# Weight blocks every 36 units instead of 34 in a fused attention and feed-forward kernel

## The chip, the cores and the metric

The kernel runs on one core of a Trainium2 chip. The metric is the device time of one execution in microseconds (us). The engines are named as in the profile: PE is TensorE (matrix products; PEld is its loading of weights), DVE is VectorE, ACT is ScalarE, POOL is GpSimd, SP is the queue of SyncE, which issues every DMA of this kernel one after the other.

## What is computed

Attention with queries averaged in pairs, then a feed-forward layer with a tanh-shrink, all in float32:

```python
B, H, S, D = 8, 8, 1152, 64                       # batches, heads, keys, head size
q_pool = q.reshape(B, H, S // 2, 2, D).mean(axis=3)
scores = np.matmul(q_pool, k.transpose(0, 1, 3, 2)) / np.sqrt(D)
scores = scores - scores.max(axis=-1, keepdims=True)
attn = np.exp(scores)
attn = attn / (attn.sum(axis=-1, keepdims=True) + 1e-09)
x = np.matmul(attn, v).transpose(0, 2, 1, 3).reshape(B * S // 2, H * D)   # 4608 x 512
h = x @ w_in                                      # w_in 512 x 2048
out = (h - np.tanh(h)) @ w_out                    # w_out 2048 x 512
```

## The kernel before

There are two stages. The first is the attention, and while it runs the weights of the second stage are prepared on engines that have time to spare. The second is the feed-forward layer, over chunks of 512 tokens; the change doesn't touch its text.

**Pairs and units.** The attention runs over 32 pairs of heads (0 to 31; four pairs make a batch). A pair has two halves of the queries, two heads and nine tiles of keys, so 36 score tiles, and each is a unit. In a unit, `score_unit` makes a tile of scores on PE (two products into `ps_s`, of which there are three buffers) and ACT writes its exponential into `p_f`. After every sixth unit, POOL adds the exponentials into `z` (`z_part`, two additions), and PE multiplies them with the values (`pv`, into `ps_o`), some units later. The sums of `z` over the keys (`z_sums`) go through `ps_s` too.

**What is made ahead.** While the units of a pair run, operands of later pairs are made. In units counted from the start of a pair (the same place in every pair from the third on): at 10 SP loads queries `q_n` and keys `kq` of the pair three ahead; at 22 POOL adds the query pairs into `kq` (`query_sums`); at 26, 28 and 30 ACT rounds `kq` to a high part `x` (`hi_part`); at 34, 0 and 2 DVE subtracts it from `kq`, which gives the low part `kq_l` (`lo_part`); at 1 SP copies the parts into the score operands `t` of the next pair, in ten DMAs (`operands`), at 6 it loads the values `v`, and at 32 it copies `x` into `bd` (`max_queries`).

**Maxima.** The maximum of every row of scores is found ahead, one to two pairs earlier, from rough products: PE writes products of `bd` and `x` into `ps_m` (two buffers), and one unit later DVE reduces each (`mx`, 14 reductions for a pair, at 13, 15, 17, 20, 22, 24, 27, 29, 31, 34, 0, 2, 5 and 7). `max_rows` then reduces them to `nm`, splits it into a rounded and a remaining part in `m2`, PE turns the result (`turn`), ACT copies it out (`mt`), and SP writes it to `m_dram` and reads it back into two rows of `t`.

**Batches.** At 12 in the first pair of the next batch the last sums of a batch are copied out (`z_out`). SP stores them (`z_dram`, at 14) and reads them back as `rec` in four DMAs (`sums`, at 18). DVE takes the reciprocals, and SP spreads them to `r_dram`.

**Weight blocks.** The two weight matrices come as 64-bit patterns of double precision. 32 blocks of 128 x 512 are turned into a high and a low float32 part on the way. `w_block` loads a block (`w_raw`, 512 KB, SP); ACT scales the upper words; five DVE operations follow (clamp, sign, shift, mask, and the lower words); POOL adds; ACT rounds to the high part; POOL subtracts to the low part; SP stores both (`w_hl` to `wi_dram` or `wo_dram`, 512 KB). The places of these steps are a table of offsets in units from the block's start.

**What sets the order.** In the first stage each engine's instructions stay in the order in which the program writes them (`InOrder`, line 27; in the profile all of them have line 37, so tiles tell them apart). The order is written by tables of units: `at` and `first` hold what is issued in each unit, `first` ahead of the unit's scores and `at` behind them. Each engine and SP then work through their own rows strictly in that order, and the first row that waits holds up the rows behind it.

Of the kernel before, what the change touches and what calls it, by code (L numbers as in the profile page):

```python
# [8 lines left out]
F32 = mybir.dt.float32  # L9
F32R = mybir.dt.float32r  # L10
I32 = mybir.dt.int32
AF = mybir.ActivationFunctionType
ALU = mybir.AluOpType
# [30 lines left out]
def kernel(  # L44
# [87 lines left out]
    op0 = ctx.enter_context(tc.tile_pool(name="op0", bufs=1))  # L132
# [3 lines left out]
    t, n = chunks.pop()  # L136
# [4 lines left out]
    with ExitStack() as actx:  # L141
# [3 lines left out]
        op = actx.enter_context(tc.tile_pool(name="op", bufs=1))  # L145
# [12 lines left out]
        U = 4 * KT  # L158
# [18 lines left out]
        at, first = {}, {}  # L177
        end = n_pair * U

        def add(u, f, *args, at=at):  # L180
            at.setdefault(u, []).append(lambda: f(*args))
# [69 lines left out]
        def max_rows(u, pi, steps):  # L251

            w = pairs[pi]
            nm = sm.tile([P, 2, 5], F32, name="nm")
            for h in range(2):
                dve.tensor_reduce(nm[:, h], w.mx[:, 4 * h:4 * h + 5], axis=AX.X, op=ALU.max, negate=True)
            m2 = sm.tile([P, 2, 2, 5], F32R, name="m2")
            dve.tensor_copy(m2[:, 0], nm)
            dve.tensor_tensor(m2[:, 1], nm, m2[:, 0].bitcast(F32), op=ALU.subtract)
            mt = sm.tile([20, P], F32R, name="mt")  # L260
            md = m_dram[w.i]

            def turn():
                ps = w.ps_t = ps_m.tile([P, 2, 512], F32R, name="ps_m")[0:20, 0, 0:P]
                pe.transpose(ps, m2.rearrange("p s h t -> p (s h t)"), ident_r)

            def out():
                act.activation(mt, w.ps_t, AF.Copy)

            def there():  # L270
                sp.dma_start(md[:, 0:10 * P].rearrange("s (r n) -> s r n", n=P), mt.bitcast(F32))

            def back():

                sp.dma_start(w.t2[64:66, :, 0:SQ].bitcast(F32), md.rearrange("s (h n) -> s h n", h=2)[:, :, 0:SQ])
            add(u + steps[0], turn)
            add(u + steps[0] + 1, out, at=first)
            add(u + steps[1], there)
            add(u + steps[2], back)
# [58 lines left out]
        def z_out(u, w, hf, ps):  # L338

            act.activation(w.z_s[:, hf.n * HQ:(hf.n + 1) * HQ], ps[:, 0:HQ], AF.Copy)  # L340
            if hf.n == 1:
                def store():
                    sp.dma_start(x_dram[w.hp, :, w.b * SQ:(w.b + 1) * SQ], w.o_s)
                    sp.dma_start(z_dram[w.b].rearrange("r h a s -> (r h) a s")[:, w.hp], w.z_s[0:P:32])
                add(u + 2, store)
                if w.hp == NP - 1:
                    add(u + 6, lambda: tot.append((w.b, sums(w.b))))
                    if w.b < B - 1:
                        add(u + 22, lambda: reciprocals(dve, *tot[0]))
                        add(u + 25, lambda: spread(sp, *tot.pop(0)))  # L350

        def sums(b):

# [7 lines left out]
        def reciprocals(eng, b, t):  # L361

            eng.scalar_tensor_tensor(t[:, 0], t[:, 0], 1e-9, t[:, 1], op0=ALU.add, op1=ALU.add)
            eng.reciprocal(t[:, 0], t[:, 0])

        def spread(dma, b, t):
            dma.dma_start(r_dram[b].rearrange("h a (x n) -> (h a x) n", n=SQ * NP * 2 // P), t[:, 0])
# [3 lines left out]
        def w_block(u, kind, r, c):  # L371

            top = float.fromhex("0x1.dffffep-96")
            raw = wp.tile([P, WB, 2], I32, name="w_raw", bufs=2)
            lo, hi = raw.bitcast(mybir.dt.uint16)[:, :, 1], raw[:, :, 1]
            ts, stt = dve.tensor_scalar, dve.scalar_tensor_tensor
            t = []

            def begin():

                t[:] = [wp.tile([P, WB], I32, name=f"w_{i}", bufs=1 + (i == 1)) for i in range(3)]
                t.append(wp.tile([P, 2, WB], F32R, name="w_hl", bufs=2))
                act.activation(whole(t[0]), whole(hi), AF.Copy, scale=2.0 ** -112)

            def whole(x):
                return x.bitcast(F32)

            def store():
                src = t[3].bitcast(F32)
                if kind == 0:  # L390
                    f = c // P
                    sp.dma_start(wi_dram[f:f + WB // P, :, :, r].rearrange("f p s m -> p s f m"),
                                 src.rearrange("p s (f m) -> p s f m", m=P))
                else:
                    sp.dma_start(wo_dram[r, :, :, c:c + WB], src)
            sp.dma_start(raw.rearrange("p n w -> p (n w)"),
                         (w_in, w_out)[kind][r * P:(r + 1) * P, 2 * c:2 * (c + WB)])
            for i, op in ((12, begin),
                          (17, lambda: ts(whole(t[0]), whole(t[0]), -top, top, op0=ALU.max, op1=ALU.min)),
                          (20, lambda: ts(t[1], t[0], -0x80000000, None, op0=ALU.bitwise_and)),  # L400
                          (22, lambda: stt(t[1], t[0], 3, t[1], op0=ALU.logical_shift_left, op1=ALU.bitwise_or)),
                          (25, lambda: ts(t[2], t[1], -0x800000, None, op0=ALU.bitwise_and)),
                          (27, lambda: stt(whole(t[2]), lo, 2.0 ** -36, whole(t[2]), op0=ALU.mult, op1=ALU.mult)),
                          (29, lambda: pool.tensor_tensor(whole(t[1]), whole(t[1]), whole(t[2]), op=ALU.add)),
                          (34, lambda: act.activation(t[3][:, 0], whole(t[1]), AF.Copy)),
                          (36, lambda: pool.tensor_tensor(t[3][:, 1], whole(t[1]), whole(t[3][:, 0]), op=ALU.subtract)),
                          (40, store)):
                add(u + i, op)

        blocks = []  # L410
# [3 lines left out]
            for r in range(f // P, (f + WB) // P):  # L414
                blocks.append((1, r, 0))
        for i, blk in enumerate(blocks):
            u = U // 2 + 34 * i
            add(u, w_block, u, *blk)

        tot = []  # L420
# [17 lines left out]
        for pi in range(n_pair):  # L438
            u = pi * U
            units = dict(load=-98, query_sums=-86, hi_q=-82, hi_k=-80, max_queries=-76, lo_q=-74, lo_k=-72, operands=-35, load_v=-30)  # L440
            row, steps = -26, (5, 8, 14)
            parts = [-60 + i * 33 // 14 for i in range(14)]
            step = 2
            if pi == 0:
                units.update(load=-70, query_sums=-60, hi_q=-59, hi_k=-58, max_queries=-57, lo_q=-56, lo_k=-55, operands=-54,
                             load_v=-50)
                row, steps, step = -32, (2, 4, 5), 0
                parts = [-46 + i for i in range(14)]
            if pi == 1:
                v0 = -U  # L450
                units.update(load=v0 - 69, query_sums=v0 - 31, hi_q=v0 - 30, hi_k=v0 - 29, max_queries=v0 - 28, lo_q=v0 - 27,
                             lo_k=v0 - 26, operands=v0 - 25)
                parts = [v0 + 2 + i * 20 // 14 for i in range(14)]
                row, steps, step = v0 + 23, (2, 4, 8), 0
            if pi == 2:
                units.update(query_sums=-80, hi_q=-76, hi_k=-74, max_queries=-70, lo_q=-66, lo_k=-64)
                parts = [-49 + i * 23 // 14 for i in range(14)]
            add(u + units["load"], load, pi)
            add(u + units["query_sums"], query_sums, pi, dve if pi < 2 else pool)
            for what, f in (("hi", hi_part), ("lo", lo_part)):  # L460
                add(u + units[what + "_q"], f, pi, 0, SQ)
                add(u + units[what + "_k"], f, pi, SQ, 2 * SQ)
                add(u + units[what + "_k"] + step, f, pi, 2 * SQ, KQ)
            add(u + units["max_queries"], max_queries, pi)
            for x, part in zip(parts, spots):
                add(u + x, max_part, u + x, pi, *part)
            add(u + units["operands"], operands, pi)
            add(u + units["load_v"], load_v, pi)
            add(u + row, max_rows, u + row, pi, steps)
# [97 lines left out]
    for ci, (t0, n) in enumerate(chunks):  # L567
        x_h, x_l, _ = xs
        po = []
        for fc in range(NF):  # L570
# [15 lines left out]
            def rest(po=po, g=g, fc=fc, t0=t0, nt=n // P, ci=ci):  # L586
                if fc == 0:
                    po += [ps_o.tile([P, DM], F32, name="ps_o") for _ in range(nt)]
                second(po, *g, nt, fc)
                if fc == NF - 1:  # L590
                    store(po, t0, nt, ci)
# [39 lines left out]
```

## Time and profile before

| what | us |
|---|---|
| median of three runs | 1827.98 |
| lowest and highest of them | 1825.22 and 1828.62 |
| the profiled execution | 1825.99 |
| its span, from the first instruction to the last | 1824.2 |
| PE busy | 1741.4 |
| DVE busy | 1403.8 |
| ACT busy | 1084.0 |
| POOL busy | 1050.4 |

The attention ends near 990 us in the span, and the feed-forward layer takes the rest. A group of instructions is shown with its count, its busy time, the mean of one in ns and the idle time of its engine just ahead of it, with what ended that idle time. In a row of the timeline the first number is the start in us, the second the length, and brackets give the idle time ahead of it and who ended it. A row of busy times in stretches has a bracketed count behind each engine's time, and then the granted PE clock, the busy share of the DMA engines, and GB/s.

### The profile page before, as it was taken

What the parts mean: (1) busy time and instruction counts of PE and PEld (TensorE: products, weight loads), DVE (VectorE), ACT (ScalarE), POOL (GpSimd) and SP (SyncE); (2) the same over time, 40 slices, a digit from 0 to 9 for tenths busy, and PEclk for the clock granted to TensorE, in tenths of its full rate; (3) what the DMA queues carried; (4) which work ended last, traced back from release to release, by engine and by line L of the source; (5) the groups of instructions that cost most, each with busy time, mean ns of one, the idle gap of its engine ahead of it and who ended that gap; (6) DMA issues with size and microseconds to landing.
All of it is one profiled execution on the core that took longest, in us unless ns stands there. A gap on an engine that the chain in (4) does not pass through costs nothing. (4 is left out here: it accounts for less than half of the span.)

```text
span 1824.2 us, 28257 instructions
## 1 busy us (share of the span) xinstructions
PE 1741.4 (95%) x9920; PEld 1306.6 (72%) x9920; DVE 1403.8 (77%) x1823; ACT 1084.0 (59%) x2473; POOL 1050.4 (58%) x756
## 2 busy tenths in 40 slices
PE   4999999999999989999998999999999999999998
PEld 3666666766676666666665777878787888788887
DVE  5776767677767777776741899988998899888897
ACT  2555555656565555555554655666666666666676
POOL 2666778777787767777864274353534444433433
PEclk9999999999999999999999999999999999999999
DMA  8767787878878676878763821020101010100000
GB/s 211 201 175 219 180 227 196 221 196 219 228 207 232 168 213 181 212 212 227 196 169 131 313 58 64 6 65 6 64 9 61 13 57 18 44 14 34 27 15 21
DMA packets 104141, 242.29 MB, mean 133 GB/s; under 512 B 18112, under 2 KB 43328, under 8 KB 104000
## 3 DMA queue, kind: packets, MB, share of 16 engines
q1 hardware_dynamic: 104000, 240.49, 47.7%
q8 instruction: 78, 1.28, 0.3%
q14 instruction: 63, 0.52, 0.1%
HBM read 109.64 MB, written 36.42 MB: 80 GB/s over the span
## 5 line engine op out<-in xcount | busy, mean ns | idle before, releaser
L37 DVE TENSOR_REDUCE mx<-ps_m 128x2 f32<-128x768 f32 x448 | 405.5, 924 | 258.2 <-PE ps_m L37 257.9
L37 ACT ACTIVATE p_f<-ps_s 128x288 f32<-128x288 f32 x1152 | 418.0, 411 | 193.6 <-PE ps_s L37 169.7
L37 PE MATMUL ps_s<-t 128*128 128x288 f32 (+1 forms) x2304 | 447.6, 313 | 15.1 <-ACT p_f L37 9.1
L544 POOL TENSOR_TENSOR g_lo<-g_s,g_hi 128x512 fp32r<-128x512 f32 (+1 forms) x160 | 209.2, 1308 | 414.3 <-ACT g_hi L543 360.0
L37 PEld LDWEIGHTS ps_s<-t 128*128 128x128 f32 (+1 forms) x2304 | 357.2, 191 | 120.0 <-issue 90.2
L37 POOL TENSOR_TENSOR z<-p_f 128x576 f32<-128x576 f32 x192 | 289.7, 1509 | 159.5 <-PE ps_s L37 112.0
L526 PE MATMUL ps_h<-x,wi 128*128 128x512 f32 (+1 forms) x1440 | 325.0, 370 | 1.4 <-DVE g_s L541 1.4
L37 PE MATMUL ps_o<-p_f,v 128*64 128x288 f32 x2304 | 325.7, 419 | 0.0
L37 POOL TENSOR_TENSOR z<-z,p_f 128x576 f32<-128x576 f32 x192 | 290.4, 1512 | 17.9 <-ACT p_f L37 3.2
L526 PEld LDWEIGHTS ps_h<-x,wi 128*128 128x128 f32 x1440 | 254.9, 188 | 53.4 <-ACT g_u L532 1.8
L551 PE MATMUL ps_o<-wo,g_hi 128*128 128x512 f32 x1008 | 275.7, 392 | 4.2 <-ACT g_hi L543 3.8
L37 PE MATMUL ps_m<-x,bd 128*128 128x384 f32 x864 | 237.7, 355 | 32.0 <-DVE mx L37 17.5
L37 PEld LDWEIGHTS ps_o<-p_f,v 128*64 128x64 f32 x2304 | 149.8, 138 | 114.8 <-issue 29.8
L551 PEld LDWEIGHTS ps_o<-wo,g_hi 128*128 128x128 f32 x1008 | 186.8, 188 | 46.3 <-ACT g_hi L543 7.4
L543 ACT ACTIVATE g_hi<-g_s 128x512 fp32r<-128x512 f32 (+1 forms) x160 | 94.3, 590 | 153.8 <-DVE g_s L542 151.5
L37 PEld LDWEIGHTS ps_m<-x,bd 128*128 128x128 f32 x864 | 143.5, 196 | 49.6 <-DVE mx L37 27.9
L539 DVE SCALAR_TENSOR_TENSOR g_w<-g_w,g_u 128x512 f32<-128x512 f32 (+1 forms) x160 | 172.6, 1079 | 0.0
L551 PE MATMUL ps_o<-wo,g_lo 128*128 128x512 f32 x504 | 160.1, 393 | 5.6 <-POOL g_lo L544 5.4
L532 ACT ACTIVATE g_u<-ps_h 128x512 f32<-128x512 f32 (+1 forms) x160 | 87.5, 547 | 119.5 <-PE ps_h L526 119.0
L542 DVE COPY_PREDICATED g_s<-g_m,g_t 128x512 f32<-128x512 int32 (+1 forms) x160 | 133.3, 833 | 14.7 <-DVE g_s L541 0.5
L540 DVE SCALAR_TENSOR_TENSOR g_w<-g_s,g_w 128x512 f32<-128x512 f32 (+1 forms) x160 | 129.3, 808 | 18.8 <-ACT g_s L534 2.2
L541 DVE SCALAR_TENSOR_TENSOR g_s<-g_s,g_w 128x512 f32<-128x512 f32 (+1 forms) x160 | 126.5, 790 | 17.0 <-ACT g_t L533 0.5
(60 smaller groups left out, 1887.8 us busy)
## 6 DMA issues: line engine op xcount, KB each, us to landing
t<-x SPq DMA_DIRECT2D x64, 432.0 KB
q_n<-in_q_dram SPq DMA_DIRECT2D x32, 576.0 KB
kq<-in_k_dram SPq DMA_DIRECT2D x32, 576.0 KB
t<-kq_l SPq DMA_DIRECT2D x64, 288.0 KB
t<-x SPq DMA_DIRECT2D x64, 288.0 KB
v<-in_v_dram SPq DMA_DIRECT2D x32, 576.0 KB
bd<-x SPq DMA_DIRECT2D x64, 144.0 KB
t<-kq_l SPq DMA_DIRECT2D x64, 144.0 KB
```

What stands on the lines that cost most here:

```text
L37: ins = self.tc.keep_in_program_order(f(*args, **kwargs))
L526: nc.tensor.matmul(h, wi[fc][:, w, c], x[:, c, 0:n], start=(j == 0), stop=(j == len(mm) - 1))
L532: nc.scalar.activation(u, h, AF.Square)
L539: nc.vector.scalar_tensor_tensor(w, w, PL, u, op0=ALU.mult, op1=ALU.mult)
L540: nc.vector.scalar_tensor_tensor(w, s2, P2, w, op0=ALU.add, op1=ALU.mult)
L541: nc.vector.scalar_tensor_tensor(s1, s1, P1, w, op0=ALU.add, op1=ALU.mult)
L542: last = nc.vector.copy_predicated(s1, m.bitcast(I32), th).ins
L543: nc.scalar.activation(g_h, s1, AF.Copy)
L544: nc.gpsimd.tensor_tensor(g_l, s1, g_h.bitcast(F32), op=ALU.subtract)
L551: nc.tensor.matmul(po[j], g[:, ts], wo[fc][:, w], start=(fc == 0 and i == 0), stop=(fc == NF - 1 and i == 2))
```

## The change

A block now starts every 36 units, the length of a pair, at unit 0 of each pair: before, it started every 34 units, from unit 18, so that its steps moved two units earlier in the pair with each block. The offsets of its steps change too. The five DVE operations now stand at 13, 15, 18, 22 and 25 of each pair, POOL's two at 27 and 32, and ACT's two at 11 and 30. The store stands at 36, which is unit 0 of the next pair, behind the load of the next block (also at unit 0) and ahead of the ten copies of the operands (unit 1).

In `max_rows` the rounding of `nm` moves from DVE to ACT, and the subtraction behind it is put three units later. `max_rows` itself starts one unit earlier, and what follows the turn keeps its place. The reciprocals of a batch move from unit 34 to 28, and their spreading from 37 to 31.

```diff
             m2 = sm.tile([P, 2, 2, 5], F32R, name="m2")
-            dve.tensor_copy(m2[:, 0], nm)
-            dve.tensor_tensor(m2[:, 1], nm, m2[:, 0].bitcast(F32), op=ALU.subtract)
+            act.activation(m2[:, 0], nm, AF.Copy)
+
+            def rest():
+                dve.tensor_tensor(m2[:, 1], nm, m2[:, 0].bitcast(F32), op=ALU.subtract)
+            add(u + steps[0] - 3 if steps[0] > 3 else u + 1, rest, at=first)
...
-                        add(u + 22, lambda: reciprocals(dve, *tot[0]))
-                        add(u + 25, lambda: spread(sp, *tot.pop(0)))
+                        add(u + 16, lambda: reciprocals(dve, *tot[0]))
+                        add(u + 19, lambda: spread(sp, *tot.pop(0)))
...
-            for i, op in ((12, begin),
-                          (17, lambda: ts(whole(t[0]), whole(t[0]), -top, top, op0=ALU.max, op1=ALU.min)),
+            for i, op in ((11, begin),
+                          (13, lambda: ts(whole(t[0]), whole(t[0]), -top, top, op0=ALU.max, op1=ALU.min)),
...
-                          (40, store)):
+                          (36, store)):
...
-            u = U // 2 + 34 * i
+            u = U * i
...
-            row, steps = -26, (5, 8, 14)
+            row, steps = -27, (6, 9, 15)
```

The next rows show what stands in three queues, around pair 21. `w_raw` is the load of a block, `wo_dram<-w_hl` the store of one, `t...` the copies of the operands.

SP, from the last copy of the operands in pair 21 on, before:

```order
L37 DMA t_0_122<-x 64x1728
L37 DMA r_dram<-rec 128x36
L37 DMA v<-in_v_dram 128x1152
L37 DMA w_raw<-in_moe_w_out_dram 128x1024
L37 DMA q_n<-in_q_dram 128x1152
L37 DMA kq<-in_k_dram 128x1152
L37 DMA x_dram<-o_s 128x576
L37 DMA z_dram<-z_s 4x576
L37 DMA wo_dram<-w_hl 128x1024
L37 DMA m_dram<-mt 2x10x128
L37 DMA t_0_122<-m_dram 2x2x576
L37 DMA bd_125<-x 64x576 x2
```

The same stretch of SP after the change:

```order
L37 DMA t_0_122<-x 64x1728
L37 DMA v<-in_v_dram 128x1152
L37 DMA q_n<-in_q_dram 128x1152
L37 DMA kq<-in_k_dram 128x1152
L37 DMA x_dram<-o_s 128x576
L37 DMA z_dram<-z_s 4x576
L37 DMA m_dram<-mt 2x10x128
L37 DMA t_0_122<-m_dram 2x2x576
L37 DMA bd_125<-x 64x576 x2
L37 DMA w_raw<-in_moe_w_out_dram 128x1024
L37 DMA wo_dram<-w_hl 128x1024
L37 DMA t_1_123<-kq_l 64x1152
```

The block's load and store have moved from among the loads of `v`, `q_n` and `kq` to a place between `bd` and the first copy of the next operands; the same two rows stand there in every pair from the second on.

POOL in pair 21, up to the query sums (`kq`), before:

```order
L37 TENSOR_TENSOR w_7341<-w_7341,w_7342 128x512
L37 TENSOR_TENSOR z<-p_f 128x576
L37 TENSOR_TENSOR z<-z,p_f 128x576
L37 TENSOR_TENSOR w_hl<-w_7341,w_hl 128x512
L37 TENSOR_TENSOR z<-p_f 128x576
L37 TENSOR_TENSOR z<-z,p_f 128x576
L37 TENSOR_TENSOR z<-p_f 128x576
L37 TENSOR_TENSOR z<-z,p_f 128x576
L37 TENSOR_TENSOR kq<-q_n 128x576
```

POOL in pair 21 from the query sums on, after the change:

```order
L37 TENSOR_TENSOR kq<-q_n 128x576
L37 TENSOR_TENSOR z<-p_f 128x576
L37 TENSOR_TENSOR z<-z,p_f 128x576
L37 TENSOR_TENSOR w_7540<-w_7540,w_7541 128x512
L37 TENSOR_TENSOR z<-p_f 128x576
L37 TENSOR_TENSOR z<-z,p_f 128x576
L37 TENSOR_TENSOR w_hl<-w_7540,w_hl 128x512
```

Before, the block's two operations on POOL stood at another place in each pair, here well ahead of the query sums; now they stand behind them in every pair.

DVE in pair 20, around the reciprocals (`rec`), before:

```order
L37 TENSOR_SCALAR w_7340<-w_7340 128x512
L37 TENSOR_REDUCE mx<-ps_m 128x2
L37 TENSOR_SCALAR w_7341<-w_7340 128x512
L37 TENSOR_REDUCE mx<-ps_m 128x2
L37 TENSOR_TENSOR kq_l<-kq,x 128x576
L37 SCALAR_TENSOR_TENSOR rec<-rec 128x36
L37 RECIPROCAL rec<-rec 128x36
L37 SCALAR_TENSOR_TENSOR w_7341<-w_7340,w_7341 128x512
L37 TENSOR_REDUCE mx<-ps_m 128x2
L37 TENSOR_TENSOR kq_l<-kq,x 128x576
```

The same place after the change:

```order
L37 TENSOR_REDUCE mx<-ps_m 128x2 x2
L37 TENSOR_SCALAR w_7194<-w_7193 128x512
L37 TENSOR_REDUCE mx<-ps_m 128x2
L37 SCALAR_TENSOR_TENSOR w_7194<-w_raw,w_7194 128x512
L37 TENSOR_REDUCE mx<-ps_m 128x2
L37 SCALAR_TENSOR_TENSOR rec<-rec 128x36
L37 RECIPROCAL rec<-rec 128x36
L37 TENSOR_REDUCE mx<-ps_m 128x2 x3
L37 TENSOR_TENSOR kq_l<-kq,x 128x576
```

The reciprocals now stand three reductions earlier, and the block's operations have left the stretch in which the low parts `kq_l` are made.

More of the change, by code (lines that the diff above doesn't have):

```diff
@@ L397, in w_block @@
                          (w_in, w_out)[kind][r * P:(r + 1) * P, 2 * c:2 * (c + WB)])
-            for i, op in ((12, begin),
-                          (17, lambda: ts(whole(t[0]), whole(t[0]), -top, top, op0=ALU.max, op1=ALU.min)),
[L400 to L406, printed above, removed]
-                          (40, store)):
+            for i, op in ((11, begin),
+                          (13, lambda: ts(whole(t[0]), whole(t[0]), -top, top, op0=ALU.max, op1=ALU.min)),
+                          (15, lambda: ts(t[1], t[0], -0x80000000, None, op0=ALU.bitwise_and)),
+                          (18, lambda: stt(t[1], t[0], 3, t[1], op0=ALU.logical_shift_left, op1=ALU.bitwise_or)),
+                          (22, lambda: ts(t[2], t[1], -0x800000, None, op0=ALU.bitwise_and)),
+                          (25, lambda: stt(whole(t[2]), lo, 2.0 ** -36, whole(t[2]), op0=ALU.mult, op1=ALU.mult)),
+                          (27, lambda: pool.tensor_tensor(whole(t[1]), whole(t[1]), whole(t[2]), op=ALU.add)),
+                          (30, lambda: act.activation(t[3][:, 0], whole(t[1]), AF.Copy)),
+                          (32, lambda: pool.tensor_tensor(t[3][:, 1], whole(t[1]), whole(t[3][:, 0]), op=ALU.subtract)),
+                          (36, store)):
                 add(u + i, op)
```

## The prediction

> **What bounds the kernel now.** I read the busy times first, then the busy times by stretch, then what PE waits for, and last the queues of SP and POOL, because the order shows rows moved there.
>
> ```profile
> span 1824.2 us, 28257 instructions
> PE 1741.4 (95%) x9920; PEld 1306.6 (72%) x9920; DVE 1403.8 (77%) x1823; ACT 1084.0 (59%) x2473; POOL 1050.4 (58%) x756
> L37 ACT ACTIVATE p_f<-ps_s x1152: 382/410/453, 38.0 to 989.8; 128x288 f32<-128x288 f32 x192
> 38.00:164.40 126.40, 119.71 (x779) 84.57 (x780) 92.40 (x112) 68.86 (x184) 82.92 (x58) 0.99 0.72 190
> 164.40:907.00 742.60, 718.50 (x4901) 502.02 (x4901) 537.33 (x671) 428.36 (x1153) 560.26 (x379) 1.00 0.78 209
> 907.00:990.20 83.20, 79.86 (x534) 53.39 (x534) 28.94 (x44) 45.55 (x128) 57.14 (x41) 0.99 0.60 164
> ```
>
> The exponentials run from 38 to 990 us: that is the attention, and the change is there. Its units are counted by them, so a pair starts at every 36th. The three stretches are pairs 0 to 3 (126.4 us), 4 to 28 (742.6 us, 29.70 each) and 29 to 31 (83.2 us). PE is busy 718.5 of 742.6 us, so PE bounds the stage, but DMA (the share ahead of the last number in a row) is close behind: 0.72 and 0.78 of its time.
>
> ```profile
> PE ps_m L37 <- DVE mx L37: 21.1, 22, 1.9
> PE ps_s L37 <- ACT p_f L37: 4.9, 14, 0.9
> 343.40:371.90 28.50, 28.33 (x197) 19.95 (x197) 20.05 (x26) 17.06 (x46) 23.14 (x16) 1.00 0.81 214
> 371.90:401.00 29.10, 28.48 (x198) 20.01 (x197) 22.53 (x28) 17.05 (x46) 23.37 (x16) 1.00 0.72 196
> 637.50:669.50 32.00, 29.15 (x199) 20.06 (x198) 22.77 (x28) 17.02 (x47) 21.37 (x16) 1.00 0.71 193
> ```
>
> From 70 to 936 us PE waits 21.1 us for maxima and 4.9 us for exponentials. The other three rows are pairs 10, 11 and 20. As a block moves two units in each pair, the run before has tried nearly every place. Pair 20, whose block falls among the low parts, takes 32.0 us; pairs 10 and 11, whose DVE operations stand between units 13 and 25, take 28.5 and 29.1.
>
> **The change, part by part.**
>
> *DVE's places.* After the change the first operations stand as in pair 11 and the last as in pair 10, so DVE should hold up PE nowhere. The block's rounding on ACT comes at unit 30, where it stood in pair 11:
>
> ```profile
> 396.10 0.68 ACT L37 ACTIVATE x<-kq 128x576 fp32r<-128x576 f32 x1
> 396.68 0.62 ACT L37 ACTIVATE w_hl<-w 128x512 fp32r<-128x512 f32 x1
> 397.65 0.83 PE L37 MATMUL ps_s<-t 128*128 128x288 f32 x4 [0.45 <-ACT p_f L37]
> ```
>
> It follows ACT's third high part directly, and PE waits 0.45 us. So this part alone would give pair 11's 29.1 us, 0.6 less than 29.70.
>
> *The rounding of the maxima.*
>
> ```profile
> L37 DVE CAST m<-nm x32: 173/902/1242, 25.4 to 941.6; 128x10 fp32r<-128x10 f32 x32
> L37 ACT ACTIVATE mt<-ps_m x32: 249/251/268, 27.0 to 946.6; 20x128 fp32r<-20x128 f32 x32
> ```
>
> DVE loses 32 operations of 902 ns in the middle case; ACT gets 32 of about 250 ns (by its nearest row). They lie in the pause in which PE does `pv` and `z_sums`, so I cost them at nothing; without that cover it would be 32 × 0.25 = 8 us. Nor do I count DVE's freed time: 29.1 us holds already that DVE stops nobody.
>
> *The load and the store of a block.* This is the part that decides. The store now stands ahead of the ten copies of the operands, and `q_n` behind them. The run before has this order in pairs 12 and 13, when pair 11's and pair 12's stores came late:
>
> ```profile
> 399.09 0.64 SPq L37 DMA_DIRECT2D wi_dram<-w_hl  x1
> 399.83 1.81 SPq L37 DMA_DIRECT2D t<-kq_l  x2
> ...
> 412.05 2.01 SPq L37 DMA_DIRECT2D q_n<-in_q_dram  x1
> 421.12 1.42 POOL L37 TENSOR_TENSOR kq<-q_n 128x576 f32<-128x576 f32 x1 [4.97 <-DMA q_n<-in_q_dram]
> 422.57 0.68 ACT L37 ACTIVATE x<-kq 128x576 fp32r<-128x576 f32 x1 [1.40 <-POOL kq L37]
> 428.06 0.52 SPq L37 DMA_DIRECT2D wo_dram<-w_hl  x1
> 449.62 1.43 POOL L37 TENSOR_TENSOR kq<-q_n 128x576 f32<-128x576 f32 x1 [2.62 <-DMA q_n<-in_q_dram]
> ```
>
> From the issue of the store to the query sums that `q_n` releases: 421.12 − 399.09 = 22.03 us, and 449.62 − 428.06 = 21.56 us; mean 21.8. POOL stands idle for 4.97 us, and ACT waits 1.40 us with exponentials queued behind it. The other half of the way, from the query sums to the next store, is POOL's own row. In pair 28 it has the order that every pair gets now:
>
> ```profile
> 895.64 1.42 POOL L37 TENSOR_TENSOR kq<-q_n 128x576 f32<-128x576 f32 x1 [3.26 <-DMA q_n<-in_q_dram]
> 897.03 1.42 POOL L37 TENSOR_TENSOR z<-p_f 128x576 f32<-128x576 f32 x1
> ...
> 899.89 1.28 POOL L37 TENSOR_TENSOR w<-w,w 128x512 f32<-128x512 f32 x1
> 901.11 1.43 POOL L37 TENSOR_TENSOR z<-p_f 128x576 f32<-128x576 f32 x1
> ...
> 903.99 1.28 POOL L37 TENSOR_TENSOR w_hl<-w,w_hl 128x512 fp32r<-128x512 f32 x1
> 905.30 0.33 SPq L37 DMA_DIRECT2D wo_dram<-w_hl  x1
> ```
>
> Seven operations without a pause, 905.30 − 895.64 = 9.66 us, and SP issues the store 0.03 us after they end. So a ring closes: store, operands, `v`, `q_n`, query sums, `z`, the block's sum, `z`, the block's low part, next store. Each step stands behind the one ahead of it in an in-order queue, and the ring is passed once per pair: 21.8 + 9.66 = 31.4 us. Before, it was open, since the block moved on in each pair. PE alone needs 29.1 us, so the ring sets the pace, and PE waits in between for ACT, which waits at unit 26 for the query sums and at unit 30 for the block's sum.
>
> How it closes in: a store 1.9 us ahead of a pair's start, as in pair 12 (399.09 against 401.0), puts the query sums at 20.1 us of the pair. POOL's sum of the block then ends 1.42 + 2.9 + 1.28 = 5.6 us later, at 25.7, but ACT comes to unit 30 near 24.8 (pair 11: 396.68 − 371.9). ACT and PE so lose 0.9 us beside the 0.45, and the pair takes 29.9. The next store comes 20.1 + 9.66 = 29.8 us after the pair's start, 0.1 ahead of the next one, and the next query sums at 21.7: ACT's high part is late too, by 1.4 + 21.7 − 21.6 = 1.5 us, since pair 12 could bear it at 21.6 (422.57 − 401.0). That pair takes 28.5 + 0.45 + 1.5 + 0.9 = 31.4, the ring's own length, and so it stays.
>
> Bounds: in pair 11 the store stands behind the ten copies; the first copy was issued at 367.90, and the query sums started at 388.51, so 20.6 us hold the same bytes in another order; with 9.66 that makes 30.3 us. The longest way is 22.03 plus pair 11's POOL part, 399.09 − 388.51 = 10.58: 32.6 us.
>
> ```profile
> 367.90 1.10 SPq L37 DMA_DIRECT2D t<-kq_l  x2
> 388.51 1.41 POOL L37 TENSOR_TENSOR kq<-q_n 128x576 f32<-128x576 f32 x1 [2.17 <-DMA q_n<-in_q_dram]
> 399.09:421.12 22.03, 21.52 (x149) 15.32 (x146) 15.69 (x23) 11.45 (x32) 12.91 (x8) 1.00 0.92 236
> ```
>
> I take 31.4, since its DMA half was measured twice in this very order. The last row says why it can't shrink much: DMA is 92% busy on that way, at 236 GB/s.
>
> The Trainium skill sees this otherwise: "DMA: Bandwidth & Descriptors", section Bandwidth, has 341 GB/s for a transfer of 1 MB. The 4.36 MB from store to `q_n` would take 12.8 us by it, an estimate, and the ring 22.4 us: it would not bind, which is the third case below. The row's 236 GB/s at 92% busy speaks against it.
>
> *The reciprocals.*
>
> ```profile
> 420.98 1.85 DVE L37 TENSOR_REDUCE mx<-ps_m 128x2 f32<-128x768 f32 x2 [1.34 <-PE ps_m L37]
> 423.10 2.42 SPq L37 DMA_DIRECT2D rec<-z_dram  x4
> 428.43 1.40 DVE L37 SCALAR_TENSOR_TENSOR rec<-rec 128x36 f32<-128x36 f32 x1
> 429.86 0.38 DVE L37 RECIPROCAL rec<-rec 128x36 f32<-128x36 f32 x1
> ```
>
> In pair 12 SP ends issuing their data at 425.52. Their new place is between the two reductions of the first row, near 421.9, so DVE would stand for 3.6 us or more, then work 1.8 us, with three reductions behind it. PE can fill its two `ps_m` buffers meanwhile, so of some 5.4 us 2 to 3.5 reach PE, seven times. Where the ring sets the pace, this fits into PE's waits or is made good in the next pair: I take 0, with 0 and 7 × 3.5 = 24 as ends. Moving them away from unit 34 gains nothing that the 29.1 us don't hold already: pair 11 has none.
>
> *Start and end.* In pair 0 the maxima of two pairs lie close together, and DVE has six reductions in a row without a pause:
>
> ```profile
> 47.27 5.27 DVE L37 TENSOR_REDUCE mx<-ps_m 128x2 f32<-128x768 f32 x6
> 976.45 1.26 DVE L37 TENSOR_TENSOR x_f<-x_f,x_r 128x512 f32<-128x512 f32 x1 [32.20 <-DMA x_r<-r_dram]
> ```
>
> Block 0's five operations now fall there. They come to some 4 us, of which I put 3 on PE (0 to 5). Its maxima are two pairs' worth, so PE's work there stays. In pairs 1 to 3 the ring closes in. Pair 1 has a store that is not late yet and two maxima more than pair 11: 29.9 us. Pair 2 takes 29.1, pair 3 between this and 31.4, so 30.6. Pair 0 takes the 32 us from 38 to 70 and the 3. At the end two blocks lie in pairs 30 and 31, where DVE otherwise stands idle for 32.20 us; the last store comes between the fetches of the first chunk: 1 us (0 to 2). The feed-forward stage keeps its work: 0, its first chunk's order differs slightly (−1 to 1).
>
> *The sum.* Pairs 0 to 3: 35 + 29.9 + 29.1 + 30.6 = 124.6 for 126.4, −1.8. Pairs 4 to 28: 25 × 31.4 = 785 for 742.6, +42.4. End: +1. That is +41.6 on the profiled execution's 1825.99 us: 1867.6. The median of the runs is 2.0 above the profiled one, so I predict 1870 us. With the ring at 30.3 and 32.6 us it would be 1842 and 1900.
>
> **The rivals.** A difference of less than 0.2% can't be told from none.
>
> *The fixed places win.* If the ring doesn't bind (the transfers go faster when nothing else is in flight) and the reciprocals find their data, pairs 4 to 28 take 29.1 us: 727.5, −15.1. With −1.8 and +1 that is −16, 1812 us. For it: pairs 10 and 11. It holds as long as store to `q_n` takes under 29.1 − 9.7 = 19.4 us; the smallest in the rows is 20.6.
>
> *The reciprocals wait, the ring doesn't.* As just now, with 7 × 2.7 = 19 us back: 1831 us, from 1819 to 1845. PE's clock makes the upper end likelier:
>
> ```profile
> 587.95 0.23 PE L37 MATMUL ps_m<-ident_r,m 128*20 128x128 f32 x1 [1.86 <-DVE mx L37]
> 588.60:592.00 3.40, 3.40 (x14) 2.15 (x16) 1.12 (x2) 1.29 (x3) 2.44 (x2) 0.50 0.98 375
> ```
>
> A pause of 1.86 us in pair 18 was followed by 3.4 us at half clock, 1.7 us more. The Trainium skill ("TensorE: Matmul & The Clock Gate", section Why this matters for your kernels) tells of drops only after pauses over about 3 us; here a shorter one did it.
>
> **How the numbers follow.** The ring 0.64, the reciprocals alone 0.14, the win 0.22. The win gives faster; the reciprocals alone split into 0.02 faster, 0.04 same, 0.08 slower. So 0.24 faster, 0.04 same, 0.72 slower. The ring's own range is 1842 to 1900. To hold eight in ten the range reaches to 1812 below, which leaves half of the win out (0.11), and to 1895 above (0.04).
>
> **What would show it.** Right: the query sums' row has 28 starts some 31.4 us apart, POOL waits for `q_n` about 4 us in every pair, ACT's high part waits for POOL, SP's store waits for POOL's `w_hl`, and PE's wait for maxima is nearly gone while that for exponentials grows from 4.9 us to over 50. Wrong: query sums 29 us apart, with little idle time ahead of them; then the DMA half was mis-sized.

## The result, and the profile after

The changed kernel takes 1868.08 us (median of 4 runs, 1867.14 to 1870.75), against 1828.30 us for the kernel before (median of 4, 1825.22 to 1831.85). The ratio is 1.0229, with a 95% interval from 1.0213 to 1.0244: the change makes the kernel 2.3% slower. The profiled execution of the changed kernel took 1867.14 us, its span 1865.0 us.

The first lines of the page of the changed kernel:

```profile
span 1865.0 us, 28261 instructions
PE 1754.3 (94%) x9920; PEld 1316.6 (71%) x9920; DVE 1385.2 (74%) x1791; ACT 1095.7 (59%) x2505; POOL 1051.7 (56%) x756
```

Its busy times by stretch (length of the stretch, busy time of each engine with its number of instructions, granted PE clock, DMA share, GB/s). The stretches are again pairs 0 to 3, 4 to 28, and 29 to 31:

```profile
38.20:167.50 129.30, 119.52 (x779) 85.60 (x780) 90.56 (x112) 70.21 (x189) 85.97 (x58) 0.99 0.71 185
167.50:946.40 778.90, 729.74 (x4902) 511.56 (x4901) 507.46 (x639) 435.92 (x1175) 556.88 (x378) 0.97 0.75 198
946.40:1029.20 82.80, 80.39 (x534) 53.48 (x534) 34.39 (x43) 46.77 (x131) 57.81 (x41) 0.98 0.60 167
```

| stretch | before, us | after, us | difference |
|---|---|---|---|
| ahead of pair 0 | 38.0 | 38.2 | +0.2 |
| pairs 0 to 3 | 126.4 | 129.3 | +2.9 |
| pairs 4 to 28 | 742.6 | 778.9 | +36.3 |
| pairs 29 to 31 | 83.2 | 82.8 | −0.4 |
| the rest of the span | 834.0 | 835.8 | +1.8 |

So the loss lies in pairs 4 to 28, now 31.16 us each. The engines hardly have more work there: DVE has 30 us less, ACT 8 us more, with the roundings of the maxima, and PE is busy 11 us longer with the same products, at a granted clock of 0.97. Above all they wait more. The waits of PE in pairs 1 to 29 (total us, times, longest):

```profile
PE ps_s L37 <- ACT p_f L37: 33.6, 35, 2.2
PE ps_m L37 <- DVE mx L37: 15.4, 7, 2.9
PE ps_m L37 <- ACT mt L37: 5.1, 29, 0.2
```

The wait for exponentials has grown from 4.9 to 33.6 us. The wait for maxima has shrunk, from 22 waits to 7: one for each batch whose reciprocals were moved. What the other engines and SP wait for, in the whole span:

```profile
POOL kq L37 <- DMA q_n<-in_q_dram: 174.7, 29, 27.3
ACT x L37 <- POOL kq L37: 54.8, 22, 8.0
DVE rec L37 <- DMA rec<-z_dram: 47.7, 7, 7.7
ACT w L37 <- DMA w_raw<-in_moe_w_in_dram: 6.2, 1, 6.2
SPq L37 <- POOL w_hl L37: 137.3, 26, 9.9
```

POOL waits 174.7 us for `q_n` (55.4 before), and SP 137.3 us for POOL's `w_hl` (39.3 before). Each of the two stands behind the other. The timeline of SP and POOL in pair 18 (which starts at 600.9) shows one round:

```profile
601.52 0.64 SPq L37 DMA_DIRECT2D wi_dram<-w_hl  x1
602.26 1.82 SPq L37 DMA_DIRECT2D t<-kq_l  x2
...
613.86 0.64 SPq L37 DMA_DIRECT2D v<-in_v_dram  x1
614.55 2.00 SPq L37 DMA_DIRECT2D q_n<-in_q_dram  x1
622.00 1.40 POOL L37 TENSOR_TENSOR kq<-q_n 128x576 f32<-128x576 f32 x1 [6.70 <-DMA q_n<-in_q_dram]
...
630.71 1.79 POOL L37 TENSOR_TENSOR w_hl<-w,w_hl 128x512 fp32r<-128x512 f32 x1
632.53 0.64 SPq L37 DMA_DIRECT2D wi_dram<-w_hl  x1
```

From a store to the query sums 622.00 − 601.52 = 20.48 us, from there to the next store 10.53, together 31.0: the pair's length.

The second part of the loss is in the seven pairs with reciprocals. In pair 20, which starts at 663.5, DVE stands 7.66 us for their data, and PE pauses twice, as the timeline of SP, DVE and PE shows:

```profile
687.12 2.90 SPq L37 DMA_DIRECT2D rec<-z_dram  x4
691.65 0.29 DVE L37 SCALAR_TENSOR_TENSOR rec<-rec 128x36 f32<-128x36 f32 x1 [7.66 <-DMA rec<-z_dram]
687.59 1.16 PE L37 MATMUL ps_s<-z,ones 128*32 128x288 f32 x12 [1.83 <-ACT p_f L37]
693.23 1.01 PE L37 MATMUL ps_m<-x,bd 128*128 128x384 f32 x2 [1.78 <-DVE mx L37]
```

From 688.9 us on PE runs at half clock for 10.2 us (the 0.50 in this row of the busy times):

```profile
688.90:699.10 10.20, 8.42 (x31) 5.80 (x31) 5.84 (x8) 3.64 (x9) 9.33 (x7) 0.50 0.52 132
```

Pairs 4, 8, 12, ... 28 take 34.7 us in the mean, the other 18 take 29.8. After a pair with reciprocals the next takes 29.1 to 29.6, since POOL and SP come ahead of PE in the long pause: the next store leaves 2.3 to 5.1 us ahead of the next pair, where the one in pair 18 left 0.7 us behind its pair's start. Then the ring closes again, and in three of the six batches the pairs are back at 31.0 to 31.6 us before the next reciprocals.

### The profile page after: what moved, and what is told of

The parts are those of the page before. It is cut to its first block, busy times and chain, and to the rows that moved or that the text cites. A ratio compares the mean times of both kernels' runs of the same rounds, so it can differ in the third digit from the quotient of the medians.

```text
span 1865.0 us, 28261 instructions
## 1 busy us (share of the span) xinstructions
PE 1754.3 (94%) x9920; PEld 1316.6 (71%) x9920; DVE 1385.2 (74%) x1791; ACT 1095.7 (59%) x2505; POOL 1051.7 (56%) x756
## 3 DMA queue, kind: packets, MB, share of 16 engines
q8 instruction: 78, 1.28, 0.3%
## 4 chain that ended last, share of the span: by engine, by line
PE 62%; DVE 10%; DMA 10%; ACT 7%; POOL 6%; issue 3%; SPq 2%; DVEq 0%; POOLq 0%; ACTq 0%
PE ps_s L37 18%; PE ps_o L37 13%; PE ps_o L554 12%; PE ps_h L529 12%; PE ps_m L37 7%; DMA q_n<-in_q_dram 3%; DMA z_dram<-z_s 2%; DVE g_s L544 2%; DVE g_s L545 2%; SPq L37 2%; DMA x_f<-x_dram 2%; ACT p_f L37 2%; DVE g_w L543 2%; POOL x L124 1%; POOL x_f L118 1%
## 5 line engine op out<-in xcount | busy, mean ns | idle before, releaser
L37 PEld LDWEIGHTS ps_s<-t 128*128 128x128 f32 (+1 forms) x2304 | 361.7, 193 | 131.9 <-issue 84.9
L37 PE MATMUL ps_o<-p_f,v 128*64 128x288 f32 x2304 | 330.8, 424 | 0.0
L37 PE MATMUL ps_m<-x,bd 128*128 128x384 f32 x864 | 243.7, 363 | 32.3 <-DVE mx L37 16.9
L37 PEld LDWEIGHTS ps_o<-p_f,v 128*64 128x64 f32 x2304 | 151.5, 139 | 118.1 <-issue 34.7
L542 DVE SCALAR_TENSOR_TENSOR g_w<-g_w,g_u 128x512 f32<-128x512 f32 (+1 forms) x160 | 180.0, 1125 | 0.0
L37 POOL TENSOR_TENSOR kq<-q_n 128x576 f32<-128x576 f32 x30 | 42.7, 1424 | 174.7 <-DMA q_n<-in_q_dram 174.7
```

The source lines that it names most:

```text
L37: ins = self.tc.keep_in_program_order(f(*args, **kwargs))
L542: nc.vector.scalar_tensor_tensor(w, w, PL, u, op0=ALU.mult, op1=ALU.mult)
```

## The experiments

The theory: the ring through SP and POOL sets the pace, and the reciprocals' waits come on top. The main rival: the reciprocals make the loss, with PE's pauses and its clock, and the ring only echoes them. The first four runs separate the two edits.

**The store behind the copies.** The ring is opened, and nothing else is touched:

```diff
-                          (36, store)):
+                          (38, store)):
```

> The changed kernel, but the store of a block stands behind the ten copies of the operands instead of ahead of them; the reciprocals stay at unit 28. The way from the store to the query sums then holds only v, q_n and kq's load, and the ring is far shorter than a pair. Ring theory (ring and reciprocals both cost, the ring more): the 18 pairs of 4 to 28 without reciprocals fall to 29.1 us each, the 7 with them to 32 to 34.5, sum 755, so 1838 us (1828 to 1848). Rival (the waits for the reciprocals' data make the whole loss, the ring is only their echo): nothing is gained beside the shift itself, 1858 to 1868 us.

Measured: 1816.51 us, ratio to the kernel before 0.9938 (0.9920 to 0.9955). Moving this one DMA gives 51.6 us, more than the theory had said and against the rival. Pairs 4 to 28 in the busy times:

```profile
163.50:893.40 729.90, 712.53 (x4902) 500.55 (x4901) 528.97 (x640) 431.91 (x1175) 563.97 (x375) 1.00 0.80 210
```

A batch's reciprocals in pair 20, which starts at 631.0, and the transfers ahead of them in the timeline:

```profile
637.89 0.65 SPq L37 DMA_DIRECT2D wi_dram<-w_hl  x1
640.02 1.17 SPq L37 DMA_DIRECT2D q_n<-in_q_dram  x1
649.14 2.41 SPq L37 DMA_DIRECT2D rec<-z_dram  x4
654.63 0.91 DVE L37 SCALAR_TENSOR_TENSOR rec<-rec 128x36 f32<-128x36 f32 x1 [3.09 <-DMA rec<-z_dram]
```

And DVE's waits for them, with SP's for `w_hl`, in the whole span:

```profile
DVE rec L37 <- DMA rec<-z_dram: 14.5, 7, 3.1
SPq L37 <- POOL w_hl L37: 8.8, 1, 8.8
```

A pair takes 29.2 us, with reciprocals or without. My 32 to 34.5 us for the former was wrong: with the ring open, SP issues the reads of `rec` 18.1 us into the pair (649.14 − 631.0) where it needed 23.6 (687.12 − 663.5), and DVE waits 14.5 us in all instead of 47.7. PE feels up to 0.8 us of it, three times. So most of the waits for the reciprocals' data was itself the ring's work: SP came late. The last row shows that the ring is open: SP waits for `w_hl` once, and no longer in nearly every pair (26 times, 137.3 us).

**The reciprocals back.** The ring stays closed; reciprocals and spreading stand at 34 and 37 again:

```diff
-                        add(u + 16, lambda: reciprocals(dve, *tot[0]))
-                        add(u + 19, lambda: spread(sp, *tot.pop(0)))
+                        add(u + 22, lambda: reciprocals(dve, *tot[0]))
+                        add(u + 25, lambda: spread(sp, *tot.pop(0)))
```

> The changed kernel, but reciprocals and their spreading back at units 34 and 37 as before the change; the store stays ahead of the ten copies. Ring theory: no long pause lets a store leave early any more, so all of pairs 4 to 28 run at the ring's length, 31.0 to 31.6 us, 775 to 790 in sum: 1862 to 1876 us, no better than the changed kernel, although the waits for the reciprocals' data are gone. Rival (the reciprocals make the loss): the pairs with them fall from 34.7 to 29.8 us like the others, 745 in sum: 1832 to 1838 us.

Measured: 1860.19 us, ratio 1.0179 (1.0158 to 1.0200). The rival's 1832 to 1838 is refuted; the time lies 2 us under the theory's range, whose pace was a little high. Its pairs 4 to 28 in the busy times:

```profile
167.80:934.10 766.30, 718.92 (x4902) 506.22 (x4901) 513.91 (x638) 436.21 (x1175) 553.29 (x376) 0.99 0.76 200
```

PE's wait for exponentials in pairs 1 to 29, and SP's for `w_hl` in the whole span:

```profile
PE ps_s L37 <- ACT p_f L37: 45.5, 49, 2.1
SPq L37 <- POOL w_hl L37: 147.6, 31, 7.0
```

And the round of pair 18 in the timeline:

```profile
595.66 0.64 SPq L37 DMA_DIRECT2D wi_dram<-w_hl  x1
608.94 1.79 SPq L37 DMA_DIRECT2D q_n<-in_q_dram  x1
616.47 1.40 POOL L37 TENSOR_TENSOR kq<-q_n 128x576 f32<-128x576 f32 x1 [7.02 <-DMA q_n<-in_q_dram]
625.18 1.80 POOL L37 TENSOR_TENSOR w_hl<-w,w_hl 128x512 fp32r<-128x512 f32 x1
627.00 0.64 SPq L37 DMA_DIRECT2D wi_dram<-w_hl  x1
```

No wait for maxima is left, and the pairs take 766.3 / 25 = 30.65 us. Over the 24 rounds in this stretch the way from store to query sums takes 20.25 us in the mean (19.3 to 21.2), and back 10.37 (10.0 to 10.6): 30.6 us. That this is the pair's length says little by itself, since every version has one store in each pair, and its rounds are as long as its pairs in the mean. What shows the closed ring is that neither half holds slack. SP comes from the store at 595.66 to `q_n` at 608.94 with no more than 0.11 us between two of its rows. POOL starts the query sums when `q_n` has landed, its seven operations leave 0.16 us idle in the mean, and the next store follows the end of `w_hl` by 0.02 us. Of the 32 stores, 31 wait for `w_hl`.

So the ring sets the pace alone here, and the changed kernel's other 7.9 us come from the reciprocals, which cost that only as long as the ring is closed: with the ring open, the next run has 1817.5 us without their move, and the one above 1816.5 with it.

**Both edits together.**

> Both edits of the two runs beside it: store behind the ten copies, reciprocals back at 34 and spreading at 37. If ring and reciprocals are the whole loss: pairs 4 to 28 take 29.1 us each, 727.5 in sum for 778.9, so 1817 us (1810 to 1823), below the kernel before. Rival (a third cause, as the DMA's load as a whole or DVE's new places): 1830 us or more.

Measured: 1817.52 us, ratio 0.9941 (0.9924 to 0.9959), as the two causes demand; no third is needed. Pairs 4 to 28 in the busy times, 29.18 us each:

```profile
164.80:894.40 729.60, 713.88 (x4903) 500.73 (x4902) 530.96 (x637) 430.50 (x1176) 565.04 (x375) 1.00 0.81 210
```

**A shorter ring.** The reciprocals are back, the store stays ahead of the copies, and `q_n` and the keys go ahead of `v` in SP's row:

```diff
-            units = dict(load=-98, query_sums=-86, ...
+            units = dict(load=-103, query_sums=-86, ...
```

> Reciprocals back at 34 and 37, store ahead of the ten copies as in the change, but q_n and the keys are loaded five units earlier, so that they stand ahead of v in SP's row. The ring stays closed but loses v's 576 KB, 2.5 us at 236 GB/s: 28.5 to 29 us, just under what PE needs. Ring theory: 1816 to 1830 us. Rival (the ring isn't what sets the pace): the same as with the reciprocals moved back alone, within 5 us.

Measured: 1814.11 us, ratio 0.9923 (0.9902 to 0.9944). Pairs 4 to 28 in the busy times:

```profile
161.20:890.30 729.10, 713.42 (x4903) 500.85 (x4902) 523.62 (x639) 431.52 (x1176) 565.01 (x376) 1.00 0.79 210
```

POOL's wait for `q_n` in one of them, by the timeline:

```profile
469.02 1.41 POOL L37 TENSOR_TENSOR kq<-q_n 128x576 f32<-128x576 f32 x1 [1.51 <-DMA q_n<-in_q_dram]
```

The way from store to query sums falls from 20.25 to 18.66 us in the mean, 1.6 us where I had expected 2.5, and the pair to 29.16, the length that it has with the ring open. The loss is gone although the store still stands ahead of the copies and SP still waits for `w_hl` 31 times (108.7 us): 766.3 − 729.1 = 37.2 us of the 46 between the medians. In the two profiled executions the rest lies at the start, where pair 0 begins 6.7 us earlier (33.2 against 39.9 us); that was not followed up.

**A longer ring, closed and open.** One more POOL addition per block, into a tile that nobody reads any more:

```diff
+                          (29, lambda: pool.tensor_tensor(whole(t[2]), whole(t[1]), whole(t[2]), op=ALU.add)),
```

With the ring closed and the reciprocals back:

> Reciprocals back and the store ahead of the ten copies, as in the run with the reciprocals moved back alone (1860 us, pairs of 30.65 us, ring 20.25 + 10.37 = 30.6 us), and one more POOL addition per block, whose result nobody reads, between the block's sum and its low part: 1.28 us by its row, inside the ring. Ring theory: the pair grows by the whole 1.28 us, to 31.9; 25 pairs give 32, so 1892 us (1880 to 1900). Rival (POOL's and SP's waits are only symptoms; POOL is idle 7 us in each pair and takes up 1.3 more): within 5 us of 1860.

Measured: 1901.72 us, ratio 1.0406 (1.0380 to 1.0432). With the ring open:

> The same added POOL operation, but with the store behind the ten copies, so the ring is open. Ring theory: POOL idles and the operation costs nothing: 1817 us (1813 to 1823). Rival (POOL's work itself is what PE waits for): 1840 us or more.

Measured: 1816.73 us, ratio 0.9943 (0.9923 to 0.9964). The stretch of pairs 4 to 28, closed and then open:

```profile
169.30:981.20 811.90, 732.54 (x4902) 516.50 (x4901) 507.72 (x638) 435.59 (x1175) 586.34 (x401) 0.97 0.71 189
```

```profile
163.70:893.00 729.30, 713.23 (x4902) 500.33 (x4901) 534.89 (x637) 430.96 (x1175) 600.93 (x401) 1.00 0.81 211
```

The same instruction costs 41.5 us in the one kernel and nothing in the other. That is the ring shown by itself: in this stretch POOL stands idle for `q_n` in both kernels, 195.5 us in the closed one and 45.0 in the open one, and still each addition counts in full where it lies ahead of the next store in the ring. It even cost more than its 1.28 us: the pair grew from 30.65 to 32.48. POOL's part of the round grew by 1.45 us (to 11.81) and the transfers' part by 0.36 (to 20.62); PE's granted clock fell from 0.99 to 0.97, with pauses of up to 5.1 us. Why the transfers' part grew isn't settled.

**The rounding alone.** The kernel before, with only the rounding of the maxima on ACT and what belongs to it:

```diff
-            dve.tensor_copy(m2[:, 0], nm)
-            dve.tensor_tensor(m2[:, 1], nm, m2[:, 0].bitcast(F32), op=ALU.subtract)
+            act.activation(m2[:, 0], nm, AF.Copy)
...
-            row, steps = -26, (5, 8, 14)
+            row, steps = -27, (6, 9, 15)
```

> The kernel before, with only the rounding of the maxima moved to ACT, the subtraction put later and the row of maxima started one unit earlier; blocks, stores and reciprocals as before. If the rounding is a part without cost: 1828 us (1822 to 1831). If DVE's freed 0.9 us per pair is what wins in the open versions: 1818 us or less. If ACT's added operation holds up exponentials: up to 8 us more, 1836.

Measured: 1819.63 us, ratio 0.9965 (0.9951 to 0.9979): between the two values, a small gain. And the opposite, the open ring with the rounding on DVE:

> Open ring and reciprocals back (1817.5 us), but the rounding of the maxima on DVE as before the change, with the subtraction right behind it and the row of maxima at its old unit. What is left of the change is the blocks' fixed places. The rounding alone gave 6 us over the kernel before. If places and rounding help PE against the same waits for maxima, fixed places need no rounding: 1817 to 1820 us. If the two add up: 1823 to 1826 us, and fixed places alone give next to nothing.

Measured: 1816.34 us, ratio 0.9942 (0.9922 to 0.9963). PE's wait for maxima in pairs 1 to 29 of the first, and pairs 4 to 28 of the second:

```profile
PE ps_m L37 <- DVE mx L37: 16.3, 18, 1.6
```

```profile
165.50:894.80 729.30, 713.54 (x4903) 500.56 (x4902) 537.13 (x663) 430.08 (x1151) 564.96 (x376) 1.00 0.80 211
```

The two parts don't add up: both go against the same waits for maxima (21.1 us before, 16.3 with the rounding alone), and where the blocks have their fixed places the rounding is worth nothing.

**A version that beats both.** Open ring, reciprocals back, and two edits at places that the traces had shown: block 0 begins at unit 18, and the block's rounding on ACT leaves unit 30, where it follows the third high part:

```diff
-                          (30, lambda: act.activation(t[3][:, 0], whole(t[1]), AF.Copy)),
-                          (32, lambda: pool.tensor_tensor(t[3][:, 1], whole(t[1]), whole(t[3][:, 0]), op=ALU.subtract)),
+                          (33, lambda: act.activation(t[3][:, 0], whole(t[1]), AF.Copy)),
+                          (34, lambda: pool.tensor_tensor(t[3][:, 1], whole(t[1]), whole(t[3][:, 0]), op=ALU.subtract)),
...
-            u = U * i
+            u = U * i if i else U // 2
```

> Open ring (store behind the ten copies), reciprocals back, and two more edits: block 0 starts at unit 18 of pair 0, so that ACT doesn't wait 5.6 us for its data there (pair 0 from 37.8 to 32 us, -5), and the block's rounding on ACT moves from unit 30 to 33, behind the pause of the exponentials, with POOL's low part at 34 (PE's 0.45 us per pair gone, 28 pairs, -13). From 1817.5 us: 1800 us (1796 to 1808). If the rounding's place isn't what PE waits for: 1812.

Measured: 1797.88 us, ratio 0.9844 (0.9821 to 0.9867): 1.6% faster than the kernel before. Its pair 0, and its pairs 4 to 28:

```profile
38.30:70.30 32.00, 31.14 (x184) 23.91 (x185) 24.67 (x30) 17.50 (x46) 18.50 (x13) 1.00 0.73 192
159.80:875.30 715.50, 711.16 (x4902) 500.25 (x4901) 509.87 (x639) 428.52 (x1175) 570.56 (x376) 1.00 0.82 215
```

Pairs of 28.62 us instead of 29.18 (14 us over 25 pairs), and pairs 0 and 1 together 64.2 us instead of 68.1 (4 us). PE is now busy 711 of 715.5 us.

## Why the prediction was right

1870 us were predicted, and 1868 measured, with the ring as the cause. By its steps:

- **DVE's places, 29.1 us per pair.** Right. With the ring open every pair takes 29.1 to 29.7 us, and the 0.45 us behind ACT's rounding at unit 30 is the one wait left beside 0.2 us for `mt` in each pair: at unit 33 it is gone.
- **The rounding of the maxima, cost 0.** Right for this change (1816.3 without it, 1817.5 with it, intervals overlapping). That it is worth 6 us by itself in the kernel before wasn't foreseen.
- **The load and the store of a block, the ring of 21.8 + 9.66 = 31.4 us.** The mechanism was right: four runs open, shorten and lengthen it, and the time follows. Both terms were off by under 8% and in opposite directions: with the ring alone, 20.25 + 10.37 = 30.6 us. POOL's part was taken from a round in which every addition took the shorter of its two times; in pair 18 after the change `w_hl` takes 1.79 us where pair 28 before had 1.28. The ring alone costs 766.3 − 742.6 = 23.7 us in pairs 4 to 28, not 42.4.
- **The reciprocals, 0 of 0 to 24.** The mis-sized term. What reaches PE is as foreseen: 15.4 us in seven waits, 2.2 each, between the 2 and 3.5 named. But they weren't absorbed. In pairs 4 to 28, PE's waits for exponentials are 43.0 us with the reciprocals back and 29.3 us with them moved, so 13.7 us are given back; but PE's clock takes 10.8 us: PE is busy 718.9 us there with the reciprocals back and 729.7 with them moved, for the same products. That is 15.4 − 13.7 + 10.8 = 12.5 us, and the two stretches differ by 778.9 − 766.3 = 12.6. By the medians it is 7.9; the profiled run with the reciprocals back was the fastest of its four (1854.98 us). With the ring open the same edit costs nothing.
- **The start, pair 0 +3.** It was +5.3 (37.33 us from 32.0), for another reason by the trace: in pair 0 PE waits for no maxima, but ACT stood 6.15 us for the block's data with exponentials behind it, and PE 3.42 us for these. Moved to unit 18, block 0 leaves pair 0 at 32.05 us; that run moves DVE's operations too, so it doesn't tell the two apart. Pairs 1 to 3 took 30.4, 30.1 and 31.6 us, 0.5 to 1.0 us more than foreseen.
- **End, +1.** +1.4 by the last two rows of the table.

So the mechanism was foreseen, but that its sum came within 2 us is luck, since the errors cancel: the ring's pace 0.75 us per pair too high (25 × 0.75 = 18.8 us), the reciprocals 8 to 13 us too low, the start 4.7 us too low. What was to be seen was seen in part: query sums 31 us apart, POOL's wait for `q_n` 5.3 us per pair (174.7 less the first 27.3, by 28) and not 4, SP behind `w_hl`. But the wait for exponentials reached 33.6 us and not 50, and that for maxima only fell to 15.4; both are the reciprocals' doing.

Of the rivals, the fixed places would have given 1812; with the ring opened they give 1816. The bound named for it, 19.4 us from store to `q_n`, fits: at 20.25 us the ring costs 1.5 us per pair, and at 18.66 us the loss is gone. The rival with the reciprocals alone (1831) is refuted from both sides, since they cost nothing without the ring and 7.9 us with it.

The Trainium skill's figure ("DMA: Bandwidth & Descriptors", section Bandwidth), by which the transfers would take 12.8 us and the ring wouldn't bind, differs from what was measured: 20.25 us. The figure is for one large transfer; here it is a row of thirteen of 144 to 576 KB, and the measurement decides. Whether the DMA engines or SP's issuing set those 20 us wasn't tried apart.

## What to carry to other kernels

Give work a fixed place in a loop, and every chain of in-order queues through it is passed once per turn: add up the way around (store, the transfers behind it, the engine they release, the way back to the store), and compare it with the turn itself. If it is longer, idle engines on it prove nothing, since an operation on an engine that was idle for some 6 us in each turn cost more than its full length; moving one DMA behind ten others was worth 2.8%. Sum up a ring's parts only from rounds in which the ring was closed: here the two parts, read from the kernel with the open ring, were 21.8 and 9.66 us, and 20.25 and 10.37 in the closed one.

## What the hardware showed beside that

- **The clock drops after short pauses, and not after all of them.** In the changed kernel's pair 20 two pauses of PE, 1.83 and 1.78 us, went with 10.2 us at half clock. Elsewhere in the same run two longer pauses of nearly the same length came out differently: behind 2.85 us in pair 12 PE ran at half clock, and behind 2.88 us in pair 16 at full clock, as the timeline and then the busy times show:

```profile
444.41 1.01 PE L37 MATMUL ps_m<-x,bd 128*128 128x384 f32 x2 [2.85 <-DVE mx L37]
567.62 0.62 PE L37 MATMUL ps_m<-x,bd 128*128 128x384 f32 x2 [2.88 <-DVE mx L37]
```

```profile
444.40:450.00 5.60, 5.59 (x20) 3.35 (x20) 4.31 (x5) 0.82 (x2) 4.89 (x4) 0.50 0.78 207
567.60:575.00 7.40, 7.38 (x49) 5.30 (x50) 7.40 (x7) 2.96 (x9) 6.34 (x6) 1.00 0.89 233
```

  So in this kernel a pause of two to three microseconds is a risk and not a price. The Trainium skill ("TensorE: Matmul & The Clock Gate", section Why this matters for your kernels) puts the bound at about 3 us; the pauses in pair 20 lie well below it.
- **POOL's additions take one of two times.** The same `z` addition of 128x576 takes 1.42 us in one place and 1.80 in another, and `w_hl` 1.28 or 1.79. The longer times are a part of why POOL's way around took 0.7 us more than forecast. In pairs 4 to 28 of the run with the reciprocals back, 70 of the 71 additions of POOL that start while DVE makes a low part (`kq_l`) take the longer time, and none of the 252 that overlap no low part. No run tried whether the low parts are the cause.
